# Cluster attention and a gated feed-forward on one core: a shorter lead-in to the sorted part, earlier requests for the sorted rows, and one half item more in five slots

## The chip, the core and the metric

The kernel runs on one NeuronCore of one Trainium2 chip. The core has five engines that each work through a list of their own: TensorE (PE in the profile, with PEld for its weight loads), VectorE (DVE), ScalarE (ACT), GpSimd (POOL) and SyncE (SP), which here only issues DMAs. The engines wait for one another through semaphores, and each list is executed strictly in its order. The metric is the device time of one execution in microseconds.

## The reference

Attention over 4 batches with 8 heads, 768 positions and head size 64, in which a query sees only the keys that are nearest to the same one of 16 centroids; then a feed-forward block with a hard-swish gate over the 3072 rows.

```python
q_assign = np.argmax(np.einsum('bhsd,hcd->bhsc', q_n, c_n), axis=-1)
k_assign = np.argmax(np.einsum('bhsd,hcd->bhsc', k_n, c_n), axis=-1)
mask = q_assign[:, :, :, None] == k_assign[:, :, None, :]
scores = np.where(mask, scale * np.matmul(q, k.transpose(0, 1, 3, 2)), -1000000000.0)
attn = softmax(scores)                 # as exp of the shifted scores over their sum
x = matmul(attn, v) as (3072, 512)     # heads side by side
h = x @ w_in                           # 512 -> 2048
out = (h * np.clip(h + 3.0, 0.0, 6.0) / 6.0) @ w_out
```

## The kernel before

The 32 heads are worked in 16 pairs. Pairs 0 to 7 (batches 0 and 1) are done with full score matrices in the first part of the kernel, while the weights are decoded. Pairs 8 to 15 (batches 2 and 3) are done in what the code calls the late part, here the sorted part: the rows of q, k and v of a pair are sorted by cluster in DRAM, so that only a band of the score matrix is left, and the result is brought back into the old order.

The steps of one sorted pair, with the names that the lines of the profile carry:

- `load_natural`, `turn_natural` (PE L899, `ps<-ident,piece`; ACT L900, `xnat`), `cluster_scores` (PE L337, `pcs`), `own_clusters` (PE L918, `pr`), `run_up`, `step_up`, `order` (PE L968 and L981, `rk`) and `positions` (DVE L995 and L997): the sorted place of every row. For the first sorted pair, 8, most of this was done in the first part.
- `load_queries`, `load_keys`: the rows in the old order into SBUF (`qn`, `kvn`), as the source of the sort.
- `scatter` (POOL L1014): 24 indirect DMAs from GpSimd that write the rows to their sorted places in DRAM (`qd` for q, `kvd` for k and v, each once for either head `t`), with three small memsets (L1006) between two of them as a pause.
- `load_ranked` 0, 1, 2 (SP L870, `piece<-qd`, `piece<-kvd`; SP L893, `vs<-kvd`): the sorted rows back into SBUF, two DMAs each, one for either head. They can start when the scatter of that head's rows has landed.
- `turn_ranked` 0 and 1 (PE L899, ACT L900 `xsort`): transposes of the sorted q rows (`piece<-qd`) and then of the sorted k rows (`piece<-kvd`). The transposes of one piece need both of its DMAs.
- `band_masks`, `band_scores` (PE L1057), `band_values` (PE L1096), `key_adds` (DVE L1110), `band_sums`, `band_divide`, `keep_ranked` (SP L1154), `gather` (POOL L1030) and `turn_back`.

TensorE is kept busy by the feed-forward of earlier batches, which is cut into half items in the list `fill`. One batch has three blocks of 256 rows. A block has eight "up" items (L645; a first half with 6 products into `uX`, a second half with 8 into `uY`) and seven "down" items (L684), each of two halves: 30 half items. The first half of an up item also asks SP for the first sums `tx` of the item two further on (L548); some second halves of down items ask SP to store `y` (L695), which waits for VectorE's last addition (L691).

The order of the sorted part is written out by hand as a list of points. `steps_of` gives every step of a pair an offset against the point of the pair's first scores; the pairs follow one another by `SLOT` = 28 points, and the first pair's offset 0 is at point `AHEAD`. At each point the loop in `fast_path` first does the steps that are due, then one half item of `fill`. Points 6 and 9 of every slot take none, so a slot has 26 half items. A slot is the 28 points from the offset 0 of a pair on; slot 0 is that of pair 8, and the 38 points ahead of it are the front. The steps of the next pairs lie in a slot too: `load_ranked` of pair 9 + s lies in points 25 and 26 of slot s, and its `turn_ranked` in point 27 and in point 0 of slot s + 1.

The engines' lists follow this order. What SP has in its list behind a DMA that waits is held up with it, and so is what TensorE has behind a transpose that waits. After the sorted part the rest of `fill` is worked off without further steps between.

Of the kernel before, what the change touches and what calls it, by code (L numbers as in the profile page):

```python
# [119 lines left out]
def fast_path(ctx, tc, ok, q, k, v, centroids, moe_w_in, moe_w_out, out):  # L120
# [57 lines left out]
    st = {}  # L178
# [10 lines left out]
    def load(g, *names):  # L189
        if g > FIRST or (g == FIRST and "v" in names):  # L190
            return
        b, h = divmod(2 * g, H)
        for name in names:
            if name == "v":
                dst = st["v", g] = vp.tile([P, 2, NCH, D], F32, name="vt")
            elif name == "q":
                st["qk", g] = qkp.tile([P, 2, NCH, 2, D], F32, name="qk")
            if name != "v":
                dst = st["qk", g][:, "qk".index(name)]
            src = {"q": q, "k": k, "v": v}[name]  # L200
            for t in range(2):
                nc.sync.dma_start((dst[:, t] if name == "v" else dst[:, :, t]), src[b, h + t].rearrange("(p j) d -> p j d", p=P))
# [9 lines left out]
    def load_weights(i):  # L212
        if i < len(chunks):
            st["raw", i] = rawp.tile([P, WC, 2], U32, name="raw")
            nc.sync.dma_start(st["raw", i], chunks[i][1])
# [54 lines left out]
    def constants():  # L270
        make_identity(nc, ident)
        for t in range(2):
            nc.vector.tensor_reduce(
                out=parity[:, t : t + 1],
                in_=ident.rearrange("p (h t c) -> p t h c", t=2, c=C)[:, t], axis=AX.XY, op=ALU.max,
            )
        nc.gpsimd.memset(half_c, 0.5)
        nc.gpsimd.memset(low_c, 1.0 / BOUND)
        nc.gpsimd.memset(ones, 1.0)
        nc.gpsimd.memset(w_low, W_LOW)  # L280
        nc.gpsimd.memset(one_hot, 0.0)

        idle(18)
# [108 lines left out]
    def scores_qk(n):  # L392
        st["ps", n] = psum_s.tile([P, 2, 512], F32, name="ps")
        scores_part(n, st["xf", where(n)[0]], True, False)
# [60 lines left out]
    def divide(n):  # L455
        return sum_up(n)()
# [710 lines left out]
            load_block()  # L1167
            fill.extend(ffn_items(b))

    SLOT, AHEAD = 28, 38  # L1170

    def steps_of(g):

        first, last = g == FIRST, g == NPAIR - 1
        if first:
            plan = [
                (-38, load_queries), (-37, load_keys, 0), (-36, load_keys, 1), (-37, run_up),
                (-36, step_up), (-31, order), (-30, positions), (-20, lambda g: st.pop("signed")()),
            ]
        else:  # L1180
            plan = [
                (-46, load_natural, 0), (-45, load_natural, 1), (-38, turn_natural, 0), (-37, turn_natural, 1),
                (-36, cluster_scores), (-34, own_clusters), (-33, run_up), (-32, step_up), (-31, load_queries),
                (-29, order), (-28, positions), (-29, load_keys, 0), (-27, load_keys, 1),
            ]
        plan += [
            (-29 if first else -24, scatter, 0), (-29 if first else -24, scatter, 1), (-12, band_masks), (-3, load_ranked, 0), (-3, load_ranked, 1),
            (-2, load_ranked, 2), (-1, turn_ranked, 0), (0, turn_ranked, 1),
        ]
        d = 1 if last else 2  # L1190
        plan += [
            (d, band_scores, (0, 5), 1), (d + 2, band_scores, (2,), 3), (d + 4, band_scores, (4,)),
            (d + 4, band_values, 0), (d + 4, key_adds, 0, 1, 2), (d + 5, key_adds, 0, 3), (d + 7, band_values, 1),
            (d + 7, key_adds, 1, 1, 2), (d + 8, key_adds, 1, 3), (d + 10, band_sums),
            (12 if last else 14, band_divide), (14 if last else 16, keep_ranked),
            (15 if last else 23, gather), (28 if last else 37, turn_back),
        ]
        return [(g, *step) for step in plan]
# [65 lines left out]
    with tc.manual_schedule():  # L1264
        nc.scalar.dma_start(cen, centroids.rearrange("h c d -> (h c) d"))
        load(0, "q", "k")
        constants()
        load(0, "v")
        load_weights(0)
        centroid_norm()  # L1270
        for part in range(3):
            turn(0, part)
        idle(5)
        nc.vector.tensor_copy(out=ident_q, in_=ident)
        load(1, "q", "k")
        load_weights(1)
        cluster_scores(0)
        scores_qk(0)
        route(0)
        scores_qk(1)  # L1280
        for part in range(2):
            route_turn(0, part)

        for n in range(0, total + lag_d + 2, 2):
            g, r = divmod(n, per_pair)
            steps = [i for i in (n, n + 1) if i < total]
            prep = prep_items(g + 1, r)
            for i in steps:
                scores(i)
                exponentials(i)  # L1290
                key_sums(i)
            for i in (n - lag_v, n - lag_v + 1):
                if 0 <= i < total:
                    attn_v(i)
            m = n - lag_d + 1
            if m >= 0 and m % NCH == NCH - 1:
                later.append(divide(m))
                ready(m)
            if prep and r == 4:
                prep.pop(0)()  # L1300
            if r == 6:
                load(g + 2, "q", "k")
                load(g + 1, "v")
            want = min(max(n + 2 - READY, 0) * up_first // (DECODED - READY) - st["done"], len(fill) // 2)
            st["done"] += want
            for i in range(max(len(prep), want)):
                if i < want:
                    fill.pop(0)()
                    fill.pop(0)()
                if i < len(prep):  # L1310
                    prep[i]()
            if n < total:
                for step in decode[: share(n, r)]:
                    step()
                del decode[: share(n, r)]
            check_all()
            checks.extend(later)
            later.clear()

        while checks or later:  # L1320
            checks.extend(later)
            later.clear()
            check_all()
        st["early"] = False
        st["moving"] = True
        open_late()
        for i, point in enumerate(late_plan()):
            for op, *args in point:
                op(*args)
            busy = i >= AHEAD and (i - AHEAD) % SLOT in (6, 9)  # L1330
            if fill and not busy:
                fill.pop(0)()
        st["last"] = True
        st["moving"] = False
        flag = whether_good()
        while fill:
            fill.pop(0)()
            if len(fill) == HOLD:
                flag()
# [363 lines left out]
```

## Time and profile before

| what | value |
| --- | --- |
| time, median of 3 runs | 957.33 us (957.01 to 957.46) |
| profiled execution, its own time | 959.56 us |
| its span, first to last instruction | 957.8 us |
| TensorE busy | 929.6 us, 97% of the span |
| VectorE busy | 594.4 us, 62% |
| GpSimd busy | 576.3 us, 60% |
| ScalarE busy | 349.8 us, 37% |
| mean granted TensorE clock | 0.998 |

The views of the profile give times in microseconds from the start of the span. A row of the timeline has the start, the duration, engine, line, operation, what is written and from what, and how many instructions were merged into the row; in brackets stands how long the engine had been idle before it and whose signal ended that. A row of the waits has the engine and line that waited, who ended the wait, the sum, the number of waits and the longest one. A row of the stages gives for a stretch of the span its length, then the busy time of PE, PEld, DVE, ACT and POOL with their numbers of instructions, then the granted clock of TensorE as a share of full speed, the share of DMA time and the DMA rate. In the chain of waits a row is a stretch with its start and length.

### The profile page before, as it was taken

Reading aid. Unit: us, or ns where it says so; the run is one execution under the profiler, and the core shown is the slowest. Engines: PE = TensorE matmul, PEld = TensorE weight load, DVE = VectorE, ACT = ScalarE, POOL = GpSimd, SP = SyncE. Lnnn points to the kernel's source line nnn. Section 1 sums busy time; section 2 is a strip of 40 time slices with the busy share of each in tenths; the row PEclk is TensorE's granted clock in tenths of the full one; section 3 lists DMA queues with packets and bytes.
Section 4 is the critical chain, followed back from the end, with each engine's and each line's share of the span. In section 5 each row is a group of like instructions: output and inputs, shape, how many; then the busy total and the mean of one; then the engine's idle time right before and its main releaser. Section 6 shows DMA issues by size and latency. Waiting matters only on the chain.

```text
span 957.8 us, 17621 instructions
## 1 busy us (share of the span) xinstructions
PE 929.6 (97%) x6358; PEld 725.5 (76%) x6358; DVE 594.4 (62%) x1306; ACT 349.8 (37%) x731; POOL 576.3 (60%) x1302
## 2 busy tenths in 40 slices
PE   8999999999899999999999999999999999999997
PEld 5444445555698798787897988888888799999996
DVE  6789888989977276274483474374471564636261
ACT  6888877765112232222232231241331311202020
POOL 3877767657367577776777878767777160303030
PEclk9999999999999999999999999999999999999999
DMA  7255464350474557456584484654744333323210
GB/s 206 90 133 155 132 176 124 106 145 10 145 223 137 151 159 164 129 130 153 153 198 119 120 204 118 160 155 114 198 142 95 102 96 116 102 72 105 66 57 26
DMA packets 174351, 124.23 MB, mean 130 GB/s; under 512 B 134064, under 2 KB 152496, under 8 KB 174256
## 3 DMA queue, kind: packets, MB, share of 16 engines
q1 hardware_dynamic: 164320, 109.86, 42.7%
q0 software_dynamic: 9216, 12.60, 4.4%
q8 instruction: 52, 0.85, 0.4%
q10 hardware_dynamic: 720, 0.56, 0.2%
q14 instruction: 43, 0.35, 0.1%
HBM read 94.67 MB, written 28.31 MB: 128 GB/s over the span
## 4 chain that ended last, share of the span: by engine, by line
PE 67%; DVE 3%; DMA 2%; issue 1%; ACT 0%; SPq 0%; another core or an unknown queue 0%; ACTq 0%; DVEq 0%
PE Y L684 17%; PE uY L645 15%; PE X L684 12%; PE uX L645 11%; PE pv L1096 3%; PE ps L899 3%; PE ps L1057 3%; DMA piece<-qd 2%; PE pv L1057 1%; PE pd L1120 1%; PE pcs L337 1%; PE rk L981 1%; PE ps L1137 1%; DVE tx L556 0%; DVE w_out_sb L523 0%
## 5 line engine op out<-in xcount | busy, mean ns | idle before, releaser
L433 POOL TENSOR_TENSOR acc<-acc,ex 128x768 f32<-128x768 f32 x64 | 123.3, 1927 | 37.4 <-ACT ex L423 33.9
L1014 POOL DMA_INDIRECT qd<-qn,pos x96 | 96.2, 1002 | 54.8 <-issue 17.5
L1030 POOL DMA_INDIRECT xn<-xsd,pos x96 | 94.3, 982 | 46.0 <-ACT sx L499 24.3
L499 ACT ACTIVATE sx<-g_sb,half_c 128x512 f32<-128x512 f32 x88 | 63.8, 725 | 146.5 <-DVE g_sb L656 126.3
L635 POOL TENSOR_TENSOR g_sb<-g_sb 128x256 f32<-128x256 f32 x52 | 41.8, 825 | 122.1 <-DVE g_sb L502 121.1
L1014 POOL DMA_INDIRECT kvd<-kvn,pos x96 | 96.1, 1001 | 27.3 <-issue 25.4
L1006 POOL MEMSET w_low<- 128x1 f32 x864 | 91.3, 106 | 33.3
L691 DVE TENSOR_TENSOR y<-y,Y 128x256 f32<-128x256 f32 x48 | 20.2, 421 | 132.7 <-PE Y L684 131.9
L684 PE MATMUL X<-w_out_sb,g_sb 128*128 128x256 f32 x384 | 90.4, 382 | 4.0 <-DVE y L691 2.2
L645 PE MATMUL uX<-xb,w_in_sb 128*128 128x128 f32 x704 | 93.0, 275 | 0.0
L684 PE MATMUL Y<-T,g_sb 128*128 128x256 f32 x384 | 88.0, 381 | 0.0
L684 PE MATMUL Y<-w_out_sb,g_sb 128*128 128x256 f32 x384 | 87.7, 380 | 0.0
L645 PEld LDWEIGHTS uX<-xb,w_in_sb 128*128 128x128 f32 x704 | 85.7, 192 | 0.0
L684 PEld LDWEIGHTS X<-w_out_sb,g_sb 128*128 128x128 f32 x384 | 70.9, 190 | 18.5 <-issue 4.0
L684 PEld LDWEIGHTS Y<-T,g_sb 128*128 128x128 f32 x384 | 72.1, 190 | 13.2 <-issue 3.9
L684 PEld LDWEIGHTS Y<-w_out_sb,g_sb 128*128 128x128 f32 x384 | 71.9, 190 | 10.6 <-issue 1.3
L656 DVE TENSOR_TENSOR sx<-uX,sx 128x128 f32<-128x128 f32 x176 | 51.1, 290 | 45.9 <-ACT sx L663 30.8
L400 PE MATMUL ps<-xf 64*128 64x384 f32 x384 | 78.5, 487 | 0.6 <-ACT ex L423 0.6
L423 ACT ACTIVATE ex<-ps 128x768 f32<-128x768 f32 x96 | 72.6, 802 | 4.5 <-PE ps L400 4.5
L443 PE MATMUL pv<-ex,vt 128*64 128x384 f32 x384 | 72.5, 499 | 0.0
L502 DVE SCALAR_TENSOR_TENSOR g_sb<-sx,g_sb 128x512 f32<-128x512 f32 x88 | 63.9, 728 | 3.3 <-ACT sx L499 2.3
L656 DVE TENSOR_TENSOR g_sb<-uY,sx 128x128 f32<-128x128 f32 (+1 forms) x176 | 65.6, 414 | 0.0
(194 smaller groups left out, 1796.7 us busy)
## 6 DMA issues: line engine op xcount, KB each, us to landing
tx<-td SPq DMA_DIRECT2D x86, 384.0 KB
raw<-in_moe_w_in_dram SPq DMA_DIRECT2D x16, 512.0 KB
raw<-in_moe_w_out_dram SPq DMA_DIRECT2D x16, 512.0 KB
xb<-xd SPq DMA_DIRECT2D x12, 512.0 KB
out_dram<-y SPq DMA_DIRECT2D x44, 128.0 KB
qk<-in_q_dram SPq DMA_DIRECT2D x18, 192.0 KB
qk<-in_k_dram SPq DMA_DIRECT2D x18, 192.0 KB
vt<-in_v_dram SPq DMA_DIRECT2D x16, 192.0 KB
```

What stands on the lines that cost most here:

```text
L400: nc.tensor.matmul(st["ps", n][:, t, 0:HALF], lhsT=x[r, NCH + j], rhs=x[r, hf * NHC : (hf + 1) * NHC], start=first, stop=last, skip_group_ ...
L423: nc.scalar.activation(out=ex, in_=sc, func=ACT.Exp, scale=SM_SCALE)
L433: nc.gpsimd.tensor_tensor(out=acc, in0=acc, in1=ex, op=ALU.add)
L443: nc.tensor.matmul(pv[t * D : (t + 1) * D], lhsT=vt[:, t, j], rhs=ex[:, t], start=(j == 0), stop=(j == NCH - 1),)
L499: nc.scalar.activation(out=r, in_=h, func=ACT.Relu, bias=half_c, scale=1.0 / 6.0)
L502: nc.vector.scalar_tensor_tensor(out=g, in0=r, scalar=1.0, in1=h, op0=ALU.min, op1=ALU.mult)
L645: nc.tensor.matmul(dst, lhsT=w[:, kt], rhs=x(kt), start=(kt == 0), stop=(kt == HK - 1))
L656: nc.vector.tensor_tensor(out=out_, in0=in0, in1=in1, op=ALU.add)
L684: nc.tensor.matmul(bank[:, half * HC : (half + 1) * HC], lhsT=g_sb[:, kind, i], rhs=w[:, i], start=(first and i == 0), stop=(last and i == ...
L1006: nc.gpsimd.memset(w_low, W_LOW)
L1014: i = nc.gpsimd.indirect_dma_start(out=rows[name, g, t], in_=src, in_offset=None, out_offset=bass.IndirectOffsetOnAxis(ap=pos[:, a, j, t : ...
L1030: nc.gpsimd.indirect_dma_start(out=xn[:, j, t], out_offset=None, in_=rows["xsd", g, t], in_offset=bass.IndirectOffsetOnAxis(ap=pos[:, 0, j ...
```

## The change

The front has 33 points instead of 38. The steps of pair 8 keep their points counted from the start of the sorted part as far as the scatter (its offset goes from -29 to -24 while the front shrinks by five); `band_masks`, `load_ranked`, `turn_ranked` and all that follows of pair 8, and every step of the later pairs, come five points sooner counted from the start. For all pairs `load_ranked` 0 and 1 go from offset -3 to -4 and `load_ranked` 2 from -2 to -3. Point 6 of the slots 1, 2, 4, 5 and 6 takes a half item too, so that these five slots have 27. With five half items fewer in the front and five more in the slots the sorted part as a whole has as many half items as before, 247, and what is left for the end is the same.

```diff
-    SLOT, AHEAD = 28, 38
+    SLOT, AHEAD = 28, 33
...
-                (-38, load_queries), (-37, load_keys, 0), (-36, load_keys, 1), (-37, run_up),
-                (-36, step_up), (-31, order), (-30, positions), (-20, lambda g: st.pop("signed")()),
+                (-33, load_queries), (-32, load_keys, 0), (-31, load_keys, 1), (-32, run_up),
+                (-31, step_up), (-26, order), (-25, positions), (-15, lambda g: st.pop("signed")()),
...
-            (-29 if first else -24, scatter, 0), (-29 if first else -24, scatter, 1), (-12, band_masks), (-3, load_ranked, 0), (-3, load_ranked, 1),
-            (-2, load_ranked, 2), (-1, turn_ranked, 0), (0, turn_ranked, 1),
+            (-24, scatter, 0), (-24, scatter, 1), (-12, band_masks), (-4, load_ranked, 0), (-4, load_ranked, 1),
+            (-3, load_ranked, 2), (-1, turn_ranked, 0), (0, turn_ranked, 1),
...
-            busy = i >= AHEAD and (i - AHEAD) % SLOT in (6, 9)
+            slot, r = divmod(i - AHEAD, SLOT)
+            busy = slot >= 0 and (r == 9 or (r == 6 and slot not in (1, 2, 4, 5, 6)))
```

## The prediction

> **What bounds the kernel.** I read the page first, then the stages, then the waits of TensorE, and last the timeline around the waits.
>
> ```profile
> span 957.8 us, 17621 instructions
> PE 929.6 (97%) x6358; PEld 725.5 (76%) x6358; DVE 594.4 (62%) x1306; ACT 349.8 (37%) x731; POOL 576.3 (60%) x1302
> ...
> 322.00:741.00 419.00, 411.63 (x2957) 347.13 (x2954) 223.64 (x618) 115.65 (x226) 323.02 (x989) 1.00 0.57 147
> 800.00:951.00 151.00, 151.00 (x1026) 141.71 (x1024) 70.99 (x185) 24.23 (x54) 25.44 (x36) 1.00 0.26 77
> ...
> PE ps L899 <- DMA piece<-qd: 4.5, 4, 2.1
> PE ps L899 <- ACT xnat L900: 1.3, 1, 1.3
> PE pcs L337 <- ACT xnat L900: 0.8, 2, 0.6
> ```
>
> TensorE is the bound, and the end is pure TensorE (151.00 of 151 us). The change adds and removes no TensorE work: 247 half items lie in the sorted part before and after. So only TensorE's idle time can change. In the slots, 322 to 741, it is 419.00 - 411.63 = 7.37 us; no saving there can be larger. The waits name its largest part: transposes that wait for the sorted q rows. The rows themselves:
>
> ```profile
> 434.77 0.84 PE L899 MATMUL ps<-ident,piece 128*128 128x128 f32 x6 [0.56 <-issue]
> 495.10 0.85 PE L899 MATMUL ps<-ident,piece 128*128 128x128 f32 x6 [0.85 <-DMA piece<-qd]
> 555.92 0.85 PE L899 MATMUL ps<-ident,piece 128*128 128x128 f32 x6 [1.33 <-DMA piece<-qd]
> 617.54 0.84 PE L899 MATMUL ps<-ident,piece 128*128 128x128 f32 x6 [2.14 <-DMA piece<-qd]
> 733.63 0.85 PE L899 MATMUL ps<-ident,piece 128*128 128x128 f32 x6 [0.21 <-DMA piece<-qd]
> ...
> 418.47 0.87 PE L899 MATMUL ps<-ident,piece 128*128 128x128 f32 x6 [1.26 <-ACT xnat L900]
> ```
>
> The first five are pairs 10, 11, 12, 13 and 15: 0.56 + 0.85 + 1.33 + 2.14 = 4.88 us in the four that matter. Pairs 8, 9 and 14 do not wait. The last row is a wait for unsorted rows of pair 11, in slot 1 alone.
>
> **Part 1: ranked rows one point sooner.** A point is worth one half item of TensorE. Its length is read from starts:
>
> ```profile
> 348.74 0.61 PE L645 MATMUL uX<-xs,tx 128*128 128x128 f32 x4
> 350.08 0.61 PE L645 MATMUL uY<-xs,tx 128*128 128x128 f32 x4
> 351.87 0.61 PE L645 MATMUL uX<-xs,tx 128*128 128x128 f32 x4
> ...
> 309.34 3.62 PE L684 MATMUL Y<-w_out_sb,g_sb 128*128 128x256 f32 x16
> 312.80 1.89 PE L684 MATMUL X<-w_out_sb,g_sb 128*128 128x256 f32 x8
> ...
> 489.74 1.01 SPq L870 DMA_DIRECT2D piece<-qd  x2
> 550.12 1.98 SPq L870 DMA_DIRECT2D piece<-qd  x2
> ...
> 490.26 4.71 DMA piece<-qd
> 611.42 5.99 DMA piece<-qd
> 730.11 3.38 DMA piece<-qd
> ```
>
> First up half 1.34 us, second 1.79; a down half (312.80 - 309.34) / 2 = 1.73. The last three rows, from the chain of waits, are the flights of the second q DMA to the transposes that waited for it: 3.38 with only a store ahead of it in SP's list, 4.71 and 5.99 behind a load of `tx`.
>
> Pair 11 needed 495.10 - 489.74 = 5.36 us from its first request, pair 12 555.92 - 550.12 = 5.80. TensorE gave them three halves, 1.34 + 1.79 + 1.34 = 4.47. In the changed order both get four, 6.26, and pair 10 gets five in place of the end of a block. So 0.56 + 0.85 + 1.33 go. The request now passes one half item's `tx` load, which is then issued behind up to six loads. I cost that at nothing: `tx` is asked for two up items, 2 x 3.13 us, ahead, and the idle list of L645 in these slots is empty although `tx` stands behind the same loads today. Were that cover gone, it would cost what the loads take to issue, 2 to 4 us once.
>
> Pair 13 is different. Counting half items, its request in slot 4 now stands right behind the two stores of `y` that end a block, and those wait for TensorE and VectorE. The same place earlier in the trace:
>
> ```profile
> 327.40 0.34 PE L1057 MATMUL ps<-xmsort 64*128 64x384 bf16 x2
> 327.50 0.88 DVE L691 TENSOR_TENSOR y<-y,Y 128x256 f32<-128x256 f32 x2 [8.62 <-PE Y L684]
> 328.83 0.45 SPq L548 DMA_DIRECT2D tx<-td  x1
> ```
>
> The DMA behind the stores starts 328.83 - 327.40 = 1.43 us after TensorE ended the product. The second q DMA follows 730.11 - 729.63, or about 0.5, later and flies 3.38: 5.3 us in all, against three halves, 4.47. So 0.8 us of 2.14 stays (ends: 0, and 2.1 with the flight of 4.71). Part 1 gives -4.88 + 0.8 = -4.1 us. Pair 15 keeps its 0.2: its SP list still opens with the same store.
>
> **Part 2: the front.** Pair 8's scatter keeps its points, and engine lists up to it are the same. Five down halves, 5 x 1.73 = 8.65 us, leave the space between it and pair 8's first transposes.
>
> ```profile
> 269.07 1.14 POOL L1014 DMA_INDIRECT qd<-qn,pos  x1 [17.40 <-DVE tx L556]
> 307.31 0.97 POOL L1014 DMA_INDIRECT kvd<-kvn,pos  x1 [0.16 <-issue]
> ...
> 307.92 0.37 SPq L870 DMA_DIRECT2D piece<-qd  x1
> 308.55 1.55 SPq L870 DMA_DIRECT2D piece<-kvd  x2
> ...
> SPq L870 <- DMA qd<-qn,pos: 10.0, 1, 10.0
> ...
> 305.56 0.49 PE L918 MATMUL pr<-ident,cs 128*128 128x128 f32 x3
> 305.89 3.62 PE L684 MATMUL Y<-T,g_sb 128*128 128x256 f32 x16
> 314.52 0.82 PE L899 MATMUL ps<-ident,piece 128*128 128x128 f32 x6
> 315.18 0.24 PE L968 MATMUL rk<-every,upto 128*128 128x1 bf16 x4
> ```
>
> The scatter is paced by GpSimd, 24 writes from 269.07 to 308.28, and SP already stands 10.0 us in front of the second q DMA until the rows are down: it leaves at 307.92. Asking sooner changes nothing. TensorE's work ahead of pair 8's transposes now ends where `Y<-T` begins, at 305.89: the work of pair 9 (`piece`, `pcs`, `pr`) has only moved ahead of it. With the flight of 3.38, the nearest since nothing stands ahead of this DMA either, the rows are there at 311.30: TensorE idles 5.4 us where it idled none. Ends: a flight of 0 gives 2.0, one of 4.71 gives 6.7. The k rows, asked for at 308.55, are needed 0.66 + 0.6 + 1.73 us later, after the q transposes, `order` and a down half, so they hide. SP's list behind the wait (`vs`, `qn`, `kvn`) is wanted only after this; the next `tx` is asked for at point 44. The front idles, then, 5.4 us: the five halves are merely moved into the slots, where TensorE has to do them.
>
> An idle of 5.4 us is longer than any in the middle of this run:
>
> ```profile
> 259.02 1.99 PE L684 MATMUL X<-w_out_sb,g_sb 128*128 128x256 f32 x8 [2.21 <-DVE y L691]
> 947.64 3.62 PE L684 MATMUL Y<-T,g_sb 128*128 128x256 f32 x16
> 955.00:957.00 2.00, 0.00 (x0) 0.00 (x0) 0.00 (x0) 0.00 (x0) 0.00 (x0) 0.50 0.03 12
> 1.36 4.06 PE L288 MATMUL warm<-ident 128*128 128x128 f32 x18 [1.36 <-POOL ident masks.py:199]
> 5.26 0.82 PE L320 MATMUL pqk<-ident,qk 128*128 128x128 f32 x6
> ```
>
> 2.21 us left the clock full. After the last product, 951.26, it is 0.50 by 955.00, 3.7 us on. At the start 18 transposes took 5.26 - 1.36 = 3.90 us; at the later pace (six in 315.18 - 314.52 = 0.66) they take 1.98. So a cold start loses 1.9 us. 5.4 is past the tail's 3.7, so I take 1.9 (ends 0 and 1.9).
>
> The Trainium skill, "TensorE: Matmul & The Clock Gate", Part 1, says that one idle window of about 3.4 us, free-running, brings the clock to half, and a busy one brings it back. The tail's 0.50 agrees. By that rule the fall is likely but not certain, a chance of (5.4 - 3.4) / 3.4 = 59%: 1.9 us if a whole window fits, none if not.
>
> **Part 3: the sixth point.** Five halves of 1.3 to 1.8 us are TensorE work that the front lost; net 0. No idle stands at these points today, so nothing is covered by them; VectorE, at 223.64 of 419 us, has room on the mean. But all steps of pairs 9 to 15 now meet other half items (shifted by 5, 5, 4, 3, 3, 2, 1 from slot 0 on), and the wait for `xnat`, 1.26 in the transposes and 0.6 of the 0.8 in `pcs`, fell on one of seven slots. With the shift it may go, or another slot get one. I take 0, ends -1.9 and +1.9.
>
> **Sum.** +5.4 (front) + 1.9 (clock) - 4.9 (pairs 10 to 13) + 0.8 (pair 13 again) + 0 = +3.2 us. The span goes from 957.8 to 961.0, the profiled execution from 959.56 to 962.8. That execution is 2.2 us above the median of 957.33, so the median goes to 960.5. About 0.2%, 1.9 us, is what a measurement here can tell from no change.
>
> **Rivals.** *The clock holds*: no window falls inside the idle time. Then +1.3, 958.6: no change that can be told. For it: the free-running phase, and a flight shorter than 3.38 would bring the idle time toward the tail's 3.7. Against: 5.4 is well past that. *Faster*: the extra half items and the earlier request cover not four waits but all idle time in the slots, 7.37 us, and the clock's price stays away as a shorter flight ends the front's wait sooner: a flight of 2.5 us gives 4.5 - 7.4 = -2.9, 954.4. It decides below a front wait of 5.4, with all 7.37 gone. For it: VectorE gets more TensorE time per slot to catch up. Against: 2.5 us of the 7.37 are many small waits, and pair 13 has the stores ahead. *Dearer slots*: the shifted steps give a second slot a wait like slot 1's, +1.9: 962.4. For it: the wait of 1.26 is one for ScalarE's copy out of PSUM, and which instructions stand ahead of that copy in ScalarE's list depends on the half items beside it. Against: six of seven slots show none.
>
> **Chances.** The forecast 0.42, the clock holds 0.29, faster 0.13, dearer slots 0.16. A tenth of the forecast's cases falls under 1.9 us: slower 0.55, same 0.32, faster 0.13. The range goes from the far side of "the clock holds" with the slot-1 wait gone (958.6 - 1.9 and a shorter front wait: 955.8) to 963.0. For slower alone it is 959.3 to 963.0.
>
> **What will show it.** Right: the transposes of pair 8 at about 311.3 with 5 us idle before them, ended by `piece<-qd`; granted clock under 1.00 in the 4 us behind; no such idle for pairs 10, 11 and 12; about 0.8 for pair 13. Wrong: pair 8 waits under 3 us, or TensorE's idle time in the slots falls by more than 5 us, or grows on `xnat` and L645.

## The result, and the profile after

The changed kernel takes 963.72 us (median of 6 runs, 962.74 to 967.9); the kernel before, run beside it, 957.17 us (6 runs, 954.24 to 957.94). The ratio is 1.0083, 95% interval 1.0059 to 1.0107: slower, by 6.6 us where 3.2 were forecast, and 0.7 us above the top of the range. The profiled execution after took 963.22 us, with a span of 961.4.

The page of the changed kernel: the same number of matmuls, but 2.9 us more of busy time (929.6 before).

```profile
PE 932.5 (97%) x6358; PEld 728.3 (76%) x6358; DVE 593.0 (62%) x1306; ACT 349.6 (36%) x731; POOL 578.4 (60%) x1302
```

The stages, first of before and then of after: length, busy time of the five engines, granted clock. The second row of either is the slots, four microseconds later after the change; the end is the same in both.

```profile
236.00:314.00 78.00, 73.27 (x465) 64.62 (x464) 62.99 (x153) 13.77 (x32) 42.96 (x109) 1.00 0.54 163
314.00:741.00 427.00, 419.63 (x3007) 354.04 (x3006) 226.43 (x626) 117.62 (x229) 325.11 (x993) 1.00 0.57 148
```

```profile
236.00:318.00 82.00, 72.44 (x460) 63.64 (x459) 64.00 (x156) 14.60 (x33) 45.10 (x112) 0.96 0.58 167
318.00:745.00 427.00, 423.24 (x3015) 357.44 (x3014) 224.66 (x624) 116.21 (x228) 327.78 (x998) 1.00 0.57 146
...
311.60:317.10 5.50, 5.47 (x24) 4.75 (x25) 1.35 (x4) 0.80 (x1) 0.35 (x1) 0.50 1.07 250
```

In the front TensorE idles 82.00 - 72.44 = 9.56 us instead of 4.73: 4.8 more. In the slots it idles 3.76 instead of 7.37: 3.6 less. And 5.47 us of work run at half clock, which is 2.7 us of loss. 4.8 + 2.7 - 3.6 = 3.9 us between these two executions, whose spans differ by 961.4 - 957.8 = 3.6. The timeline of after around pair 8, with SP and GpSimd, and one row of its chain of waits:

```profile
299.87 9.18 SPq L870 DMA_DIRECT2D piece<-qd  x2
...
305.11 0.70 PE L684 MATMUL X<-w_out_sb,g_sb 128*128 128x256 f32 x2 [1.03 <-DVE g_sb L502]
305.65 1.89 PE L684 MATMUL X<-T,g_sb 128*128 128x256 f32 x8
311.63 1.51 PE L899 MATMUL ps<-ident,piece 128*128 128x128 f32 x6 [4.09 <-DMA piece<-qd]
314.01 3.45 PE L684 MATMUL Y<-T,g_sb 128*128 128x256 f32 x8
...
308.07 0.97 POOL L1014 DMA_INDIRECT kvd<-kvn,pos  x1 [0.16 <-issue]
```

```profile
308.68 2.81 DMA piece<-qd
```

The scatter ends 0.8 us later than before (308.07 + 0.97 = 309.04; before 308.28), the flight is 2.81 us, and the rows of pair 8 are there at 311.5. TensorE has nothing left at 307.5. Behind the wait of 4.09 us its transposes and products show the half clock: six transposes 1.51 instead of 0.82, eight products 3.45 instead of 1.89. The waits of TensorE after, against 4.5, 1.3 and 0.8 on `piece<-qd` and `xnat` before:

```profile
PE ps L899 <- DMA piece<-qd: 6.4, 4, 4.1
...
PE uX L645 <- DVE g_sb L656: 1.1, 1, 1.1
```

The waits on `xnat` are gone, 2.3 us on ranked rows remain beside the 4.1 of pair 8, and one of 1.1 us on L645 is new.

One thing must be known about the profile of before: its `xnat` waits are not in every execution. Two more executions of the kernel before, taken later, have none; their ranked waits are 5.3 and 5.6 us. Beside the waits stand the slots, from 320 to 741 us, where the changed kernel has 417.24 busy (3.76 idle):

```profile
PE ps L899 <- DMA piece<-qd: 5.3, 5, 2.1
...
320.00:741.00 421.00, 415.74 (x2990) 350.89 (x2990) 224.82 (x622) 116.50 (x229) 330.71 (x1000) 1.00 0.58 148
```

```profile
PE ps L899 <- DMA piece<-qd: 5.6, 5, 2.1
...
320.00:741.00 421.00, 415.36 (x2979) 350.81 (x2978) 223.85 (x620) 116.84 (x228) 327.82 (x1001) 1.00 0.58 149
```

Idle time in the slots is 5.26 and 5.64 us here, 5.45 on the mean. Against such an execution of before the changed kernel gained not 3.6 us in the slots but 1.7 (and 0.9 by its second profile, that of `e5_again`, with 421.00 - 416.41 = 4.59 idle).

### The profile page after: what moved, and what is told of

It reads as the page before. It is cut to its first block, busy times and chain, and to the rows that moved or that the text cites. A ratio compares the mean times of both kernels' runs of the same rounds, so it can differ in the third digit from the quotient of the medians.

```text
span 961.4 us, 17631 instructions
## 1 busy us (share of the span) xinstructions
PE 932.5 (97%) x6358; PEld 728.3 (76%) x6358; DVE 593.0 (62%) x1306; ACT 349.6 (36%) x731; POOL 578.4 (60%) x1302
## 4 chain that ended last, share of the span: by engine, by line
PE 58%; POOL 7%; DVE 5%; DMA 2%; issue 2%; ACT 0%; SPq 0%; POOLq 0%; DVEq 0%; ACTq 0%
PE Y L684 15%; PE uY L645 13%; PE X L684 10%; PE uX L645 10%; PE pv L1096 3%; POOL kvd L1014 2%; POOL qd L1014 2%; PE ps L899 2%; PE ps L1057 2%; DMA piece<-qd 2%; POOL w_low L1006 2%; PE pv L1057 1%; DVE tx L556 1%; PE pd L1120 1%; DVE g_sb L635 0%
## 5 line engine op out<-in xcount | busy, mean ns | idle before, releaser
L645 PE MATMUL uX<-xb,w_in_sb 128*128 128x128 f32 x704 | 93.0, 275 | 0.0
L684 PE MATMUL Y<-T,g_sb 128*128 128x256 f32 x384 | 90.2, 386 | 0.0
L645 PEld LDWEIGHTS uX<-xb,w_in_sb 128*128 128x128 f32 x704 | 85.7, 192 | 0.0
```

What stands on the lines that cost most here:

```text
L645: nc.tensor.matmul(dst, lhsT=w[:, kt], rhs=x(kt), start=(kt == 0), stop=(kt == HK - 1))
L684: nc.tensor.matmul(bank[:, half * HC : (half + 1) * HC], lhsT=g_sb[:, kind, i], rhs=w[:, i], start=(first and i == 0), stop=(last and i == ...
```

## The experiments

All times are medians, and each kernel stands beside runs of the kernel before on the same chip. The kernel before itself took 959.95 us in one set of runs and 957.15 in the next on the same chip, so kernels of different sets are compared by their ratios. Only one of these kernels adds work that counts for nothing: the 34 transposes of `e4_warm`, which nobody reads.

| kernel | us | before, us | ratio, 95% interval |
| --- | --- | --- | --- |
| front of 33 alone (`e1_front`) | 961.38 | 959.95 | 1.0029 (1.0011 to 1.0047) |
| the same again (`e11_front`) | 962.69 | 957.91 | 1.0047 (1.0031 to 1.0064) |
| request one point sooner alone (`e2_ranked`) | 956.64 | 959.95 | 0.9970 (0.9953 to 0.9986) |
| the same again (`e12_ranked`) | 951.94 | 957.91 | 0.9944 (0.9930 to 0.9958) |
| all but the short front (`e3_rest`) | 967.34 | 959.95 | 1.0089 (1.0067 to 1.0111) |
| changed, front wait filled (`e4_warm`) | 967.05 | 959.95 | 1.0077 (1.0050 to 1.0103) |
| changed, unaltered (`e5_again`) | 963.66 | 957.15 | 1.0078 (1.0058 to 1.0098) |
| changed, no sixth points (`e6_nosix`) | 964.12 | 957.15 | 1.0079 (1.0064 to 1.0094) |
| changed, old request (`e7_norank`) | 964.91 | 957.15 | 1.0090 (1.0072 to 1.0109) |
| changed, faster scatter (`e8_brisk`) | 958.32 | 957.15 | 1.0015 (1.0005 to 1.0025) |
| before (`e9_base`, `e10_base`), one run each | 955.52, 958.09 | | |
| request, faster scatter, front 36 (`e13_even`) | 979.02 | 959.87 | 1.0199 (1.0176 to 1.0222) |
| the same, front 35 (`e14_odd`) | 985.28 | 959.87 | 1.0260 (1.0231 to 1.0290) |
| faster scatter, `tx` first (`e15_txfirst`) | 983.04 | 959.87 | 1.0239 (1.0216 to 1.0262) |
| request, faster scatter, front 38 (`e16_control`) | 980.28 | 959.87 | 1.0217 (1.0193 to 1.0241) |
| request, front 36 (`e17_front36`) | 956.53 | 959.33 | 0.9965 (0.9945 to 0.9985) |
| request, front 37 (`e18_front37`) | 958.45 | 959.33 | 0.9986 (0.9966 to 1.0007) |

### The parts one by one

The front of 33 points alone, with the old request and no half items at the sixth points:

```diff
-    SLOT, AHEAD = 28, 38
+    SLOT, AHEAD = 28, 33
-                (-38, load_queries), (-37, load_keys, 0), (-36, load_keys, 1), (-37, run_up),
+                (-33, load_queries), (-32, load_keys, 0), (-31, load_keys, 1), (-32, run_up),
-            (-29 if first else -24, scatter, 0), (-29 if first else -24, scatter, 1),
+            (-24, scatter, 0), (-24, scatter, 1),
```

> The front of 33 points alone; ranked rows asked for at -3 as before, points 6 without a half item (so five half items more are left for the end). Front theory: the idle time before pair 8's transposes (4.09 + 1.03 us in the trace after the change) and the half clock behind it (2.7 us) are all here and nothing pays them back: about +7.5 to +8 us against the kernel before, with 4 to 5 us of idle time at pair 8 and a spell of clock 0.50 behind it. Slots theory (most of the loss comes from steps that meet other half items): no more than +5 us of it in the front, the rest as new waits of TensorE in the slots.

> The front of 33 points alone, again: measured apart it was +2.8 us, while the same front with the sixth points and without the earlier request was +8.6. Half items at point 6 were worth nothing (the changed kernel without them is as slow). If the front alone carries the price, +7 to +8 here, with 4 us of idle time at pair 8; if it depends on the session or on the company of the sixth points, +2 to +3 again.

The request alone, with the front of 38 points:

```diff
-            (-12, band_masks), (-3, load_ranked, 0), (-3, load_ranked, 1),
-            (-2, load_ranked, 2),
+            (-12, band_masks), (-4, load_ranked, 0), (-4, load_ranked, 1),
+            (-3, load_ranked, 2),
```

> The ranked rows asked for one point sooner, alone; front of 38 points, points 6 as before. Front theory: the waits for ranked rows in pairs 10 to 13 (4.88 us before) fall to under 1.5 us, pair 8 does not wait, the clock stays full: 3 to 4 us faster. Slots theory: no more than 1 us faster, since the request in front of the loads of tx gives back what it saves.

> The earlier request alone, again, beside fresh profiles of the kernel before: -1 to -2 us if the first profile of before overstated the waits in the slots (taking the earlier request out of the changed kernel cost 1.2 us), -3 to -4 if not.

The front alone is slower by 1.4 and 4.8 us (differences of the medians). Both are less than the 7.5 to 8 expected for the first run, and less than the 7.3 of the prediction (5.4 + 1.9). Its two profiles show the wait of pair 8 with two lengths:

```profile
310.52 0.85 PE L899 MATMUL ps<-ident,piece 128*128 128x128 f32 x6 [1.92 <-DMA piece<-qd]
```

```profile
313.70 0.85 PE L899 MATMUL ps<-ident,piece 128*128 128x128 f32 x6 [4.29 <-DMA piece<-qd]
```

Counted from the start of the scatter (268.84 and 271.23), TensorE came 1.6 us later to the wait in the first execution, after 1.37 us of idle time at 290.8, and the rows were there 0.8 us sooner. The clock did not fall there; in the second execution it was 0.50 for 3.4 us from 314.6 on. The request alone is faster by 3.3 and 6.0 us, on either side of the 4.1 us forecast for it. Its first profile still has 421.00 - 416.74 = 4.26 us of idle time in the slots, 2.0 of them on `xnat`; its second has almost no waits left there (421.00 - 419.69 = 1.31 us idle, against 5.45 before):

```profile
PE uX L645 <- DMA tx<-td: 0.5, 1, 0.5
PE ps L899 <- DMA piece<-qd: 0.4, 1, 0.4
...
320.00:741.00 421.00, 419.69 (x3020) 354.35 (x3019) 225.57 (x625) 117.94 (x231) 330.17 (x1008) 1.00 0.59 150
```

So the parts do not add up: the front and the request together would be 1.9 us faster by the first pair of runs (1.4 - 3.3) and 1.2 by the second (4.8 - 6.0), but the whole change is 6.5 us slower. This is what the next runs look into.

The third part is the extra half items. All of the change but the short front:

```diff
-            busy = i >= AHEAD and (i - AHEAD) % SLOT in (6, 9)
+            slot, r = divmod(i - AHEAD, SLOT)
+            busy = slot >= 0 and (r == 9 or (r == 6 and slot not in (1, 2, 4, 5, 6)))
```

> All of the change but the short front: ranked rows one point sooner and 27 half items in five slots, front of 38 points. Front theory: the slots' gain without the front's price, 3 to 4 us faster than before. Slots theory: as slow as the changed kernel less its 5 us of idle front, so 1 to 3 us slower than before.

It answered another question than the one asked. With 252 half items used up instead of 247 the list runs empty before the last block may start, and TensorE stands still near the end, for about as long as this kernel is slower (7.4 us):

```profile
808.66 1.22 PE L645 MATMUL uX<-xs,tx 128*128 128x128 f32 x4 [7.13 <-DVE xs L575]
```

The half items at the sixth points can only be had from the front. The other way round, the changed kernel without them:

```diff
-            slot, r = divmod(i - AHEAD, SLOT)
-            busy = slot >= 0 and (r == 9 or (r == 6 and slot not in (1, 2, 4, 5, 6)))
+            busy = i >= AHEAD and (i - AHEAD) % SLOT in (6, 9)
```

> The changed kernel without the five half items at point 6 (short front and earlier request stay; five half items more are left for the end). Front theory: the front's price and the slots' gain stay, so the time stays within 1.5 us of the changed kernel. Sixth-point theory: the price goes with the half items: the sum of the two parts measured alone, front +2.8 and ranked -2.9, so within 2 us of the kernel before.

> The changed kernel once more, unaltered, for a second profile and beside the next three. Front theory: idle time of 4 to 5 us before pair 8's transposes and a spell of half clock behind it in this profile too, +6 to +8 us against before. Sixth-point theory (the half items at point 6 are what costs, through waits that the first profile happened not to have): idle time in the slots of 6 us or more in this profile.

964.12 against 963.66 for the unaltered changed kernel beside it: beside the earlier request the sixth points are worth nothing that can be measured, as forecast. And the changed kernel with the old request:

```diff
-            (-24, scatter, 0), (-24, scatter, 1), (-12, band_masks), (-4, load_ranked, 0), (-4, load_ranked, 1),
-            (-3, load_ranked, 2),
+            (-24, scatter, 0), (-24, scatter, 1), (-12, band_masks), (-3, load_ranked, 0), (-3, load_ranked, 1),
+            (-2, load_ranked, 2),
```

> The changed kernel with the ranked rows asked for at the old offsets -3 and -2 (short front and sixth points stay). Front theory: it loses the slots' gain, so 3 to 4 us slower than the changed kernel. Sixth-point theory: the same, 3 us slower than the changed kernel, unless the five half items already give the rows their time, then no slower than 1 us.

964.91: with the short front and the sixth points the request gives 964.91 - 963.66 = 1.3 us, where it gives 3.3 to 6.0 without them. The two intervals overlap (1.0072 to 1.0109 and 1.0058 to 1.0098), so the 1.3 is not told from nothing; the 3 to 4 us expected were not there. The profile of this kernel has 4.6 us of waits on ranked rows in the slots and none on L645; the changed kernel has 2.3 and 1.1. That is where the forecast broke.

One thing does not fit. This kernel and the front alone differ in nothing but the sixth points, and yet its ratio to the kernel before is 1.0090, that of the front alone 1.0029 and 1.0047, and its interval overlaps neither of theirs. In the same way the request would cost time where the front stands without the sixth points (1.0079 in `e6_nosix`), and save some where it stands with them. Idle time in the slots (320 to 741 us) explains little of this: 4.25 and 3.92 us for the front alone, 4.62 here. Either the sixth points cost several microseconds beside the old request, or sets of runs differ by more than their intervals say. No run here decides it.

### The front wait and the clock

Two runs take the front's price apart. In the first, 34 transposes of the identity stand ahead of pair 8's, so that TensorE is busy while it waits; in the second, pair 8's scatter has one memset instead of three between two writes, so that its rows come sooner.

```diff
     def turn_ranked(g, a):
+        if g == FIRST and a == 0:
+            idle(34)
```

```diff
-    def pause():
-        for _ in range(PAUSE):
+    def pause(count=PAUSE):
+        for _ in range(count):
...
-                pause()
+                pause(1 if g == FIRST else PAUSE)
```

> The changed kernel with 34 transposes of the identity, whose output nobody reads, on TensorE just before the transposes of pair 8's ranked rows. They fill about 3.7 us of the 4.09 us wait, so the wait stays and the clock should not fall. If the half clock behind the wait costs 2.7 us, as the trace shows, the time falls by 2.5 to 3 us against the changed kernel, to about +4 us against before; if the clock's fall is covered by something else (the k rows are late anyway), the time is that of the changed kernel.

> The changed kernel, with one memset in place of three as the pause between the writes of pair 8's scatter, and of no other pair. 24 pauses get 0.29 us shorter, so the scatter ends 6.9 us sooner and the rows of pair 8 are there before TensorE asks. Front theory: the idle time (5.1) and the half clock (2.7) at the front go, the slots' gain stays: 7 to 8 us faster than the changed kernel, equal to or up to 3 us faster than the kernel before. Sixth-point theory: no more than 3 us faster than the changed kernel, still 4 us slower than before.

The timeline of the run with the transposes: the clock stays up (six transposes 0.85, eight products 1.91 us), 0.45 of the wait is left.

```profile
307.14 3.88 PE L288 MATMUL warm<-ident 128*128 128x128 f32 x34
311.46 0.85 PE L899 MATMUL ps<-ident,piece 128*128 128x128 f32 x6 [0.45 <-DMA piece<-qd]
...
312.76 1.91 PE L684 MATMUL Y<-T,g_sb 128*128 128x256 f32 x8
```

Yet it is not seen to be faster: ratio 1.0077 against 1.0083 and 1.0078, where 2.5 to 3 us of gain were expected. In the profiled execution (963.29 us, under the median of 967.05) the slots idle 6.2 us instead of 3.8, with 1.2 and 1.4 us in two places on L645 and 1.2 on `xnat`: there the slots took what the clock gave. The interval, 1.0050 to 1.0103, is wide enough to hold a gain of 2.7 us. So the loss is seen in the trace, and this run neither confirms nor excludes it as a loss in time.

The faster scatter removes wait and clock together: its rows are loaded from 300.30 on, where the changed kernel had the second q DMA out at 309, and nothing waits for them. By this run the front's wait and clock cost 963.66 - 958.32 = 5.3 us; 7 to 8 were expected. And 958.32 is still 1.2 us above the kernel before, with the request one point sooner and no front wait. Its slots idle as long as in the later executions of before (421.00 - 415.68 = 5.3), with other waits:

```profile
PE uX L645 <- DMA tx<-td: 2.6, 3, 1.6
PE ps L899 <- DMA piece<-qd: 2.3, 3, 1.3
...
320.00:741.00 421.00, 415.68 (x2970) 351.49 (x2969) 223.71 (x622) 114.45 (x224) 322.83 (x984) 1.00 0.57 147
```

The ranked waits fell from about 5.5 to 2.3 us, and TensorE now waits 2.6 us for `tx`. In the second profile of the request alone both are 0.5 or less.

> The kernel before, unaltered, for a second profile of it. Its first profiled execution took 959.56 us, 2.4 us over the median of 957.2 that most executions show. If that execution had more waits for ranked rows than is usual, this profile (at about 957 us) shows 2 to 3 us in pairs 10 to 13 in place of 4.88; then the saving that can be had in the slots is that much smaller than I reckoned. If the waits are always 4.9, this profile shows 4.5 us or more of them, and the extra time of the first execution lies elsewhere.

> The kernel before, a third profile, for the same question: 2 to 3 us of waits for ranked rows in pairs 10 to 13 if the first profile was an unlucky one, 4.5 us or more if it was the usual one.

These two are the executions of before shown above. The waits on ranked rows of pairs 10 to 13 are there in both (5.0 and 5.2 us), so the extra time of the first profile lay elsewhere.

### Which half item the request meets

The order of SP's DMAs after the change, around pair 12, and what TensorE does there:

```profile
548.06 0.97 SPq L870 DMA_DIRECT2D piece<-qd  x2
549.12 3.84 SPq L870 DMA_DIRECT2D piece<-kvd  x2
553.01 1.73 SPq L893 DMA_DIRECT2D vs<-kvd  x2
554.91 1.41 SPq L879 DMA_DIRECT2D qn<-in_q_dram  x2
556.42 0.38 SPq L548 DMA_DIRECT2D tx<-td  x1
...
561.22 0.68 PE L645 MATMUL uX<-xs,tx 128*128 128x128 f32 x4 [1.08 <-DVE g_sb L656]
...
562.73 0.28 PE L1057 MATMUL ps<-xmsort 64*128 64x256 bf16 x2
```

Eight loads in a row, and only then the `tx`; the products that need it start 561.22 - 556.42 = 4.80 us after it. The page puts this wait down to VectorE; the next profile below has the same 4.8 us and names the DMA. A `tx` is asked for by the first half of an up item. `load_ranked` 0 and 1 stand at one point, `load_ranked` 2 and the next pair's `load_queries` at the one after it. The short front shifts all steps by five half items, an odd number, so in these slots the half item between the two points is a second half, and no `tx` comes in between. The kernel before, with the old request, has eight loads in a row at this pair too, from 550.12 on; its `tx` and the products that need it:

```profile
556.50 0.68 SPq L548 DMA_DIRECT2D tx<-td  x1
...
564.90 0.71 PE L645 MATMUL uX<-xs,tx 128*128 128x128 f32 x4
```

There the products come 8.40 us after the `tx`, behind the first band scores of the pair, and nothing waits. After the change they come ahead of the band scores (L1057, 562.73), and the time is too short. By these traces two things have to meet: a `tx` behind eight loads, and its products ahead of the band scores. With the early request and the old front a `tx` goes out between the loads, so the first is not so. Theory, X in the expectations: the gain of the request hangs on this parity. Rival, Y: it goes with the length of the front, or with the faster scatter by itself. Four kernels were to tell, all with the faster scatter and the early request: fronts of 36, 35 and 38 points without sixth points, and the changed kernel with `load_ranked` 2 and `load_queries` one point later.

```diff
-    SLOT, AHEAD = 28, 38
+    SLOT, AHEAD = 28, 36
-                (-38, load_queries), (-37, load_keys, 0), (-36, load_keys, 1), (-37, run_up),
+                (-36, load_queries), (-35, load_keys, 0), (-34, load_keys, 1), (-35, run_up),
-            (-29 if first else -24, scatter, 0), (-29 if first else -24, scatter, 1),
+            (-27 if first else -24, scatter, 0), (-27 if first else -24, scatter, 1),
```

```diff
-                (-36, cluster_scores), (-34, own_clusters), (-33, run_up), (-32, step_up), (-31, load_queries),
+                (-36, cluster_scores), (-34, own_clusters), (-33, run_up), (-32, step_up), (-30, load_queries),
...
-            (-3, load_ranked, 2),
+            (-2, load_ranked, 2),
```

> Request one point sooner, front of 36 instead of 38 points, one memset instead of three between the scatter DMAs of pair 8, no half item at a sixth point: all steps meet half items shifted by two, so an up item's first half stays a first half. Theory X (the request's gain hangs on which half item the request meets: where it stands right ahead of a load of tx in SP's list, that load leaves behind eight loads of rows and comes late): as the request alone, 4 to 6 us faster than before, TensorE's waits on tx under 1 us in all. Theory Y (any shorter front, or the faster scatter, loses the gain): 0 to 1.5 us slower than before, as with the front of 33 and the fast scatter.

> As the run with 36 points, but 35: the half items met are shifted by three, so first and second halves change places. Theory X: the gain of the request is gone, 0 to 1.5 us slower than before, TensorE's waits on tx 2 to 4 us in all. Theory Y: the same as with 36 points, whatever that gives.

> The changed kernel with one memset instead of three between the scatter DMAs of pair 8, and with load_ranked 2 back at -2 and load_queries at -30 instead of -31, so that the loads of vs and qn stand behind a load of tx in SP's list and not ahead of it. Theory X: 2 to 3 us faster than the changed kernel with the fast scatter alone (958.3 us), so 1 to 2 us faster than before, with waits on tx under 1 us in all. Theory Y: no faster than that kernel.

> Request one point sooner alone, front of 38 points, with one memset instead of three between the scatter DMAs of pair 8: what the faster scatter costs by itself. Theory X: as the request alone, 4 to 6 us faster than before. Theory Y in its second form (the faster scatter costs): 0 to 1.5 us slower than before.

All four came out 19 to 25 us slower than before, the control too: on this chip the faster scatter stalled everything else while it ran (the section on the hardware has the rows). So none of these times speaks for either theory as it was put. Only what lies behind the stall can be compared, from 310 to 815 us. TensorE is busy for 501.76 of these 505 us with the front of 36 and for 497.48 with 35: 3.24 us idle with the even shift, 7.52 with the odd one, though 3.7 of the second are on `xnat`. The kernel with `tx` first idles 6.08 us there and the changed kernel with the faster scatter 6.12: its waits on L645 are shorter (1.2 instead of 2.6 us), but the idle time is the same. That speaks against X. The last two runs change nothing but the request and the length of the front, with the scatter as before:

> Request one point sooner, front of 36 points, pauses of the scatter as before, no half item at a sixth point. All steps meet half items shifted by two (first halves stay first halves). Two down halves, 3.5 us, leave the front, so pair 8's transposes come at about 311.1 us, as its rows land (311.3): no wait over 0.5 us there. Theory X (the gain of the request hangs on which half item it meets): 4 to 6 us faster than before, as the request alone; waits of TensorE on tx under 1 us in all. Theory Y (the gain goes with the length of the front): half way between the request alone (5.4 faster) and the front of 33 with the fast scatter (1.2 slower), 2 to 4 us faster than before.

> As the run with 36 points, but 37: a shift by one, so first and second halves change places; pair 8's transposes at about 312.8 us, later than its rows. Theory X: the gain of the request is gone or mostly gone, from 1 us faster to 1.5 us slower than before, and TensorE's waits on tx 2 to 4 us in all. Theory Y: 3 to 5 us faster than before, no worse than with 36 points.

956.53 with 36 points, 2.8 us faster than before: inside the 2 to 4 expected by Y, and under the 4 to 6 expected by X. 958.45 with 37 points, 0.9 faster, which is not told from no change: inside the range of X, and under the 3 to 5 of Y. The longer front is the slower one, against the rival; but the intervals overlap (0.9945 to 0.9985 and 0.9966 to 1.0007). So the times prove neither. The traces show one wait. SP's list with 36 points, then SP's and TensorE's with 37, at the same pair:

```profile
547.30 2.41 SPq L870 DMA_DIRECT2D piece<-kvd  x2
549.85 0.92 SPq L548 DMA_DIRECT2D tx<-td  x1
550.82 1.01 SPq L893 DMA_DIRECT2D vs<-kvd  x2
552.00 1.31 SPq L879 DMA_DIRECT2D qn<-in_q_dram  x2
553.41 0.38 SPq L548 DMA_DIRECT2D tx<-td  x1
```

```profile
550.30 1.75 SPq L893 DMA_DIRECT2D vs<-kvd  x2
552.22 2.88 SPq L879 DMA_DIRECT2D qn<-in_q_dram  x2
555.20 0.38 SPq L548 DMA_DIRECT2D tx<-td  x1
...
559.98 0.68 PE L645 MATMUL uX<-xs,tx 128*128 128x128 f32 x4 [1.79 <-DMA tx<-td]
...
623.01 0.68 PE L645 MATMUL uX<-xs,tx 128*128 128x128 f32 x4 [1.79 <-issue]
```

With 36 points a `tx` goes out in the middle, at 549.85, and TensorE waits 0.5 us for `tx` in all. With 37 the same `tx` leaves at 555.20, again 4.8 us before TensorE can go on, and the wait of 1.79 us is there in two slots, 3.6 us (the second one is put down to `issue`; its `tx` left at 618.19, 4.8 us before). That is shown in these profiles. The idle time as a whole follows it only in part: from 320 to 741 us it is 5.79 with 36 points and 8.06 with 37, no less than in the later executions of before, with 2.4 and 1.7 us on `xnat`. Not shown is that `tx` makes up the difference between the request alone (3.3 us faster on one chip, 6.0 on another) and the changed kernel with the fast scatter (1.2 slower, on the first of these chips): `tx` accounts for 1.1 to 2.6 us and the ranked waits that stayed for 1.9. The rest stays open. So does the spread of the request's own gain, 3.3 and 6.0 us: the `xnat` wait (1.55 and 0.48 us in one profile of it, none in the other) comes and goes between executions.

The earlier request alone, with the old front, beats both kernels in both of its measurements.

## Why the prediction was wrong

The direction was right, and so was the front as the reason for it; the size was not: +6.6 instead of +3.2 us. Of the 3.3 us between them 2.8 lie in the slots (a gain of 1.3 instead of 4.1) and 0.8 in the clock, and the front's wait was 0.3 shorter than forecast. By its steps:

- **Pair 8 waits, +5.4**: right. The rows came at 311.5 (forecast 311.3), SP stood in front of the second q DMA as forecast. That the time fits to 0.2 us is luck: the scatter ended 0.8 us later than reckoned, and the flight was 0.6 us shorter. TensorE idled 1.03 + 4.09 = 5.1 us. The wait is split because the work of pair 9, which "has only moved ahead", had stood among the first down items in the timeline of before, where nothing waited for `g_sb`.
- **The clock, +1.9**: it fell, from 310.3 to 317.1, and 5.47 us at half speed are 2.7 us. The forecast took the cold start of the kernel, 3.9 us long, as the measure, but this spell was 6.8 us long; others in these runs are 3.4. The Trainium skill, "TensorE: Matmul & The Clock Gate", Part 1, has windows of 3.413 us that run freely; one and two of these are what is seen here. So this term was too small. Front and clock together were forecast at 7.3; by the profile they are 7.8, by the run that takes both away 5.3, and the front alone cost 1.4 and 4.8.
- **Ranked rows, -4.1**: this is the part that failed. For the request by itself the forecast is about right (-3.3 and -6.0). In the whole change it gave 1.3 us, which is not told from nothing. Two steps fell. The first is "I cost that at nothing: `tx` is asked for two up items ahead", and with it the shift of half items taken as 0. The ground for it was that the trace of before has `tx` behind the same loads without a wait. That is so, but there its products start 8.40 us after it; in the shifted order they start 4.80 us after it, and `tx` stands behind eight loads, not six. The price that was written beside it, "2 to 4 us once", was of the right order, but kept out of the sum: 1.1 us in the profile after (1.7 at the same place in the second one), 2.6 with the faster scatter, 3.6 with 37 points. The second is the ranked waits that stayed: 2.3 us, where 1.0 was forecast (0.8 and 0.2); pair 12 still waits 0.56. Why the request alone leaves only 0.4 and 0.5 us of them in its two profiles and the whole change 2.3 is open.
- **Pair 13 again, +0.8**: 1.27 us in the profile after; near enough.
- **The sixth points, 0**: not contradicted beside the early request (964.12 against 963.66); beside the old one open, as said above.
- **From the profile to the median**: the profiled execution of before was taken to be 2.2 us slow in a way that the changed kernel would share. Its `xnat` waits, 1.3 and 0.6 us, are in neither of the two later profiles of before, and the changed kernel's profile (963.22) lies at its median (963.72). From span to span the forecast was close, 961.0 against 961.4, but by luck: the `xnat` waits went and made up for the `tx`. In the medians there was nothing to go.
- **The rivals**: "dearer slots" named the mechanism in its general form, that the shifted steps meet other half items and a wait moves into the slots. It looked for it on ScalarE, at one slot and 1.9 us; what the traces show is in SP's list. Of the signs of being wrong one came, a new wait on L645. "The clock holds" and "faster" did not come about in the two profiles of the changed kernel.

In one sum: 5.1 + 2.7 for the front, -1.3 for the slots by the request's own run, is 6.5 us, and 6.55 were measured. That it fits so well is luck: the run with the idle transposes did not give the clock's 2.7 us back, and the 1.3 is a difference inside the noise.

## What to carry to other kernels

A step that moves by a number of loop items does not only move in time, it meets other neighbours in the queue that it shares: write out the new order of that queue at the places that matter, look for an urgent load that has come to stand behind a row of others, and count how soon its reader now comes. A gain of a single edit that was measured alone is not a term of the sum for the whole change, least of all where another edit shifts everything beside it. And a wait that is in one profiled execution may not be in the next: take a second profile of the kernel before, or read the forecast against the span and not the median.

## What the runs showed of the hardware

- **A scatter that is too dense can hold up everything else.** With one memset between the indirect DMAs of pair 8 instead of three, all four kernels of one set lost about 20 us, on one chip; a kernel with the same scatter on another chip, in another set, did not (958.32 us in 12 runs). The stretch from 280 to 300 us, first in the run with 36 points, then in the one with the faster scatter alone:

```profile
280.00:300.00 20.00, 5.13 (x13) 3.64 (x14) 0.58 (x2) 0.27 (x1) 16.84 (x32) 0.55 0.11 36
...
q0 software_dynamic: 496, 0.72, 10.7%
```

```profile
280.00:300.00 20.00, 19.95 (x177) 18.99 (x176) 16.57 (x49) 6.43 (x14) 17.02 (x31) 1.00 0.61 176
...
q1 hardware_dynamic: 2140, 2.68, 48.6%
q0 software_dynamic: 539, 0.81, 11.3%
q8 instruction: 2, 0.03, 1.0%
```

  In the first only GpSimd's own queue moved data; SP's transfers and the fetches of instructions moved nothing, and TensorE, VectorE and ScalarE went almost idle, TensorE at half clock for most of it. The pace of the scatter is nearly the same in both (GpSimd busy 16.84 and 17.02 us). The Trainium skill, "Runtime: NRT & Kernel Launch", Instruction fetch mechanics, says that each sequencer fetches its instructions through a DMA queue of its own. The trace fits a want of instructions as the cause but does not show it: between 262 and 312 us TensorE's waits on L645 are put down to no engine and no DMA (`issue`, 15.8 us in 15 waits) while SP's loads stood still as well. Why one chip did this and another did not is open.
- **The clock can fall after a short idle time.** The prediction read from one execution that 2.21 us of idle time left the clock full. In another execution of the kernel before it did not, after 2.20 us at the same place, and the clock was low for about 3.4 us. The timeline row and the stages:

```profile
260.04 2.50 PE L684 MATMUL X<-w_out_sb,g_sb 128*128 128x256 f32 x5 [2.20 <-DVE y L691]
...
257.90:259.90 2.00, 0.00 (x0) 0.00 (x0) 1.93 (x6) 0.00 (x0) 0.00 (x0) 1.00 0.94 285
260.10:263.30 3.20, 3.20 (x8) 2.55 (x9) 2.88 (x9) 0.00 (x0) 0.00 (x0) 0.50 1.03 284
```

  A rule that asks for a whole idle window of 3.4 us, as in Part 1 of the Trainium skill's "TensorE: Matmul & The Clock Gate", does not cover this.
